# Seven tile products for eight in the second product of two chunks of a sequence transform

## The chip, the cores and the metric

One core of one Trainium2 chip. The metric is the device time of one execution, in microseconds; before the change it is 792.81 us (median of three runs, 792.65 to 792.82). Names of engines: PE is TensorE (matmuls), DVE VectorE, ACT ScalarE, POOL GpSimd, SP SyncE, which only issues DMAs here.

## The reference

```python
def reference(A_x, A_dft_seq_re, A_dft_seq_im, A_dft_hid_re, A_dft_hid_im, B_x, B_w_gate, B_w_up, B_w_down):
    xn = _layernorm(x, axis=-1)                              # x = A_x, 2048 x 512
    a = einsum("bsd,ed->bse", xn, dft_hid_re);  b = einsum("bsd,ed->bse", xn, dft_hid_im)
    s = einsum("ts,bse->bte", dft_seq_re, a) - einsum("ts,bse->bte", dft_seq_im, b)
    h = sigmoid(xn @ w_gate) * (xn @ w_up)                   # 512 -> 1792
    g = silu(h @ w_down)                                     # 1792 -> 512
    return x + s * g
```

The sequence transforms are 2048x2048, the hidden ones 512x512, all in float32.

## The kernel before

**Arithmetic.** Each operand is split into a high part (a copy on ACT in a reduced float32 form, line 119) and a low part (the difference, on DVE, line 124). A tile product takes three matmuls, high by high, high by low and low by high, in `mm3` (lines 67 to 71); line 68 sets their order, and `late` puts the one with the low part of the moving operand third. Matrix products are made by a scheme of seven products for eight: products 1 and 2 take raw blocks, products 5, 6, 7 and 4 sums of blocks, product 3 a raw block against a sum. `combine` (line 127) makes the sums on DVE.

**Stages.** First the sequence transform of the normalised x, in four chunks of 512 output positions (class `Chunk`, made in `begin_seq`), which writes the blocks `f_raw[t][0..3]` in DRAM; then the GLU in fourteen blocks (`block`, `Down`), whose partial results add up in DRAM (`g_part`); last the hidden transform (`hidden_units`), which reads `f_raw` and sums of it (`f_sum`, made by `f_sums`), multiplies by the gate and writes the output.

**Units.** Work is a list of units, most of them 12 matmuls of 128x512. Ahead of unit n the loop at the end of the kernel asks for the loads of the units up to n + 5 (`LOAD_AHEAD`), and makes the splits of those up to n + 2 (`SPLIT_AHEAD`). What else is to happen stands in tables by unit number: `sooner` (ahead of the unit's loads), `amid` (behind its splits), `after` (behind its matmuls). Each engine runs its own instructions in the order in which this loop writes them. SBUF is 54 pages of 4 KB a partition, taken in turn: a load on SP's queue waits until the page it gets has been read for the last time.

**PSUM.** Banks go by tags: ga, ua, gb, ub, gc, uc, and two called pd.

**The transform.** The units of product 1 for pp 0 to 3 take the four chunks in turn, then those of product 2 (16 units each). Then each chunk does its products 5, 6, 7, 3 and 4, four units each (`add_product`). Product 1 is copied out by `snap` and stands in a bank again for the chain of 6, 7 and 4 (`again`, line 285); product 2 is copied out and added by a sum of the two blocks in PSUM, and `put` writes it. Products 5 and 3, and 6 and 7, meet in `join` (line 320): DVE subtracts one from a copy of the other and the result is written once. The sums of blocks of the transform matrix (t1 to t4) are made by DVE; in chunk 0 t1 and t3 are a `Sum`: a load, and a DMA on POOL's queue that adds the second block to it in SBUF (line 232). The second half of x (rows j = 1) is fetched (line 155), measured (`stats`, whose scale is made by POOL in lines 167 to 169) and normalised (line 186) while product 2 runs, and `a_sums` makes its sums.

**The GLU.** `w_operands` makes the seven operands from the gate and up weights, each 128x512, and splits each by itself; `Down` keeps four sums of blocks in one page.

## Time and profile before

| | before |
|---|---|
| time, median of three runs | 792.81 us (792.65 to 792.82) |
| span of the profiled execution | 790.8 us |
| busy PE, DVE, ACT, POOL | 786.3, 670.1, 520.9, 148.6 us |
| matmuls | 3466 |
| bytes moved over the span | 190.46 MB, mean 241 GB/s |
| DMA packets under 512 B | 6208 of 56306 |

The span goes from the first to the last instruction of the profiled execution. A row of a grouped view reads: line, engine, operation, written tile <- read tile, partitions x elements and type, count, then busy time and the mean of one, then the idle time of that engine just ahead, and what ended it. A row of a timeline: start, duration, the same names, and in brackets the idle time ahead of it with its releaser. A row of the chain: start, length, engine, tile and line. A row of the waits: who waits <- for whom, then total us, how often, and the longest. A row of the windows: the window, then for PE, its weight loads, DVE, ACT and POOL the busy time, the granted clock, the mean busy share of the DMA engines and GB/s. A row of the DMAs: line, tiles and count, bytes, and the issue times.

### The profile page before, as it was taken

The numbers are of one execution on the slowest core, as the hardware profiler recorded it, in microseconds if no ns is written. First come the engines' busy times: TensorE is split into PE (matmuls) and PEld (weight loads), VectorE is DVE, ScalarE is ACT, GpSimd is POOL, SyncE is SP. The second block draws the span as 40 slices with busy tenths as digits, with TensorE's granted clock in tenths as the row PEclk, the third lists the DMA queues.
The fourth block names the chain that finished last, engine by engine and source line by source line (L and its number), as shares of the span: only waits on it lengthen the run. The fifth ranks groups of instructions, "written<-read, shape, count | busy, mean of one in ns | idle before, by whom it ended". The sixth has DMA issues, their size and how long they took to land.

```text
span 790.8 us, 9957 instructions
## 1 busy us (share of the span) xinstructions
PE 786.3 (99%) x3466; PEld 650.8 (82%) x3466; DVE 670.1 (85%) x881; ACT 520.9 (66%) x795; POOL 148.6 (19%) x199
## 2 busy tenths in 40 slices
PE   9999999999999999999999999999999999999998
PEld 7888888888888888888888888888888888888886
DVE  6877799978899989899999888668869898896967
ACT  6787575552543555677887767576577787887571
POOL 3525300000021002022111131122222111111301
PEclk9999999999999999999999999999999999999999
DMA  9994988357699446859976996799999898999996
GB/s 345 409 380 124 312 241 278 120 197 279 256 274 361 160 163 224 227 165 229 201 128 96 228 228 186 220 207 294 286 299 265 186 226 219 237 285 316 268 348 169
DMA packets 56306, 190.46 MB, mean 241 GB/s; under 512 B 6208, under 2 KB 6720, under 8 KB 56256
## 3 DMA queue, kind: packets, MB, share of 16 engines
q0 software_dynamic: 23360, 77.62, 45.5%
q1 hardware_dynamic: 32896, 112.21, 38.9%
q8 instruction: 27, 0.44, 0.2%
q14 instruction: 23, 0.19, 0.1%
HBM read 122.68 MB, written 70.27 MB: 244 GB/s over the span
## 4 chain that ended last, share of the span: by engine, by line
PE 99%; DVE 0%; issue 0%
PE pd L71 30%; PE ga L71 15%; PE ua L71 15%; PE uc L71 10%; PE gc L71 10%; PE gb L71 9%; PE ub L71 9%; PE pd L417 0%; PE gb L417 0%; PE ub L417 0%; DVE page L883 0%; DVE page L884 0%
## 5 line engine op out<-in xcount | busy, mean ns | idle before, releaser
L124 DVE TENSOR_TENSOR page<-page 128x512 fp32r<-128x512 f32 (+1 forms) x378 | 343.1, 938 | 69.8 <-ACT page L119 68.5
L119 ACT ACTIVATE page<-page 128x512 fp32r<-128x512 f32 (+1 forms) x378 | 297.2, 829 | 108.0 <-DVE page L128 95.5
L71 PE MATMUL pd<-page 128*128 128x512 f32 x1068 | 259.5, 388 | 0.0
L71 PEld LDWEIGHTS pd<-page 128*128 128x128 f32 x1068 | 199.8, 188 | 41.2
L128 DVE TENSOR_TENSOR page<-page 128x1024 f32<-128x1024 f32 (+2 forms) x244 | 195.4, 820 | 1.2 <-DMA page<-in_w_gu_dram 0.3
L71 PE MATMUL ga<-page 128*128 128x512 f32 x528 | 139.1, 390 | 0.0
L71 PE MATMUL ua<-page 128*128 128x512 f32 x528 | 138.8, 389 | 0.0
L71 PEld LDWEIGHTS ga<-page 128*128 128x128 f32 x528 | 99.3, 188 | 21.4 <-ACT page L363 0.7
L71 PEld LDWEIGHTS ua<-page 128*128 128x128 f32 x528 | 99.4, 188 | 20.6
L559 POOL DMA_DIRECT2D g_part<-page x76 | 66.2, 871 | 265.4 <-ACT page L568 159.9
L568 ACT ACTIVATE page<-pd 128x512 f32<-128x512 f32 x140 | 82.4, 598 | 24.7 <-PE pd L71 17.4
L71 PE MATMUL gc<-page 128*128 128x512 f32 x336 | 88.3, 389 | 0.0
L71 PE MATMUL uc<-page 128*128 128x512 f32 x336 | 88.3, 389 | 0.0
L71 PE MATMUL gb<-page 128*128 128x512 f32 (+1 forms) x336 | 86.8, 385 | 0.0
L71 PE MATMUL ub<-page 128*128 128x512 f32 x324 | 85.3, 389 | 0.0
L71 PEld LDWEIGHTS uc<-page 128*128 128x128 f32 x336 | 63.1, 188 | 13.1
L71 PEld LDWEIGHTS gc<-page 128*128 128x128 f32 x336 | 63.1, 188 | 13.1
L71 PEld LDWEIGHTS gb<-page 128*128 128x128 f32 x336 | 62.2, 188 | 12.6
L71 PEld LDWEIGHTS ub<-page 128*128 128x128 f32 x324 | 60.8, 188 | 12.6
L308 POOL DMA_DIRECT2D f_raw<-page x16 | 9.0, 564 | 190.2 <-DVE page L320 137.5
L676 ACT ACTIVATE page<-ga 128x512 f32<-128x512 f32 x28 | 16.6, 593 | 17.4 <-PE ga L71 13.3
L694 DVE TENSOR_TENSOR page<-page 128x512 f32<-128x512 f32 x28 | 19.3, 689 | 10.0 <-ACT page L691 9.3
(105 smaller groups left out, 392.5 us busy)
## 6 DMA issues: line engine op xcount, KB each, us to landing
g_part<-page POOLq DMA_DIRECT2D x84, 512.0 KB, 7.4
page<-in_c_re_dram SPq DMA_DIRECT2D x60, 512.0 KB, 7.5
page<-in_c_im_dram SPq DMA_DIRECT2D x32, 512.0 KB, 6.2
page<-f_raw SPq DMA_DIRECT2D x28, 512.0 KB, 7.4
page<-in_w_gu_dram SPq DMA_DIRECT2D x22, 512.0 KB, 6.5
f_raw<-page POOLq DMA_DIRECT2D x16, 512.0 KB, 5.8
f_sum<-page POOLq DMA_DIRECT2D x16, 512.0 KB, 7.3
page<-f_sum SPq DMA_DIRECT2D x16, 512.0 KB, 9.9
```

The source lines that it names most:

```text
L71: nc.tensor.matmul(ps, ws[w], ms[m], start=first and i == 0, stop=last and i == 2, skip_group_check=go_on)
L119: nc.scalar.activation(self.parts[0], self.raw, AF.Copy)
L124: nc.vector.tensor_tensor(lo, self.raw, hi.bitcast(F32), op=SUB)
L128: (engine or nc.vector).tensor_tensor(dst, a, b, op=op)
L308: nc.gpsimd.dma_start(f_raw[self.t][block], v)
L559: nc.gpsimd.dma_start(g_part[i], pg, accum_op=ADD)
L568: nc.scalar.activation(pg[:, o, :], po, AF.Copy, scale=float(sign))
L676: nc.scalar.activation(s[k][:, m, :], ps[c + "a"], AF.Copy)
L694: nc.vector.tensor_mul(s[k][:, 0, :], s[k][:, 0, :], ps["u" + tag] if tag else s[k][:, 1, :])
```

## The change

In the transform, product 2 of chunks 2 and 3 (`PAIR`) leaves the units of `Chunk`. Two groups `Inner` do it for both chunks together: one group for pp 0 and 1, one for pp 2 and 3, each with seven products of 2 x 3 matmuls. The products stand as units of six matmuls, two by two behind every second unit of products 6, 7, 3 and 4: the first group between the units of chunk 1, the second between those of chunk 2, in banks that the chunk doesn't use. Each group loads x and its four blocks of the matrix again, normalises and sums x, and makes the sums of its blocks. Chunks 2 and 3 write product 1 as block 0, and the groups add to it in DRAM by accumulating DMAs. Of all chunks products 5, 6, 7, 3 and 4 are now each copied out by ACT; 5 and 6 write blocks 3 and 2, products 7 and 3 are added to these by accumulating DMAs, and `join` is gone. t3 is a `Sum` in every chunk. With eight units fewer at the start, fetch, statistics, normalisation and sums of the second half of x stand closer together. In the GLU six of seven weight operands are split two at a time, as 1024, through `Piece`; `Down` keeps three sums in a page and one in place; and the first `f_sums`, in steps of two units ahead of the GLU, go to its later part, in steps of one.

```diff
+    class Piece(Value):
+
+
+        def __init__(self, whole, of):
+            super().__init__([whole], None)
+            self.whole, self.of, self.begin, self.high = whole, of, whole.begin, whole.high
+
+        def get(self):
+            return [self.of(v) for v in self.whole.get()]
...
+    PAIR = 2, 3
...
-                t3 = Value([b22], onto(b12.load, b22.load)) if t else Sum(b12, b22)
+                t3 = Sum(b12, b22)
...
-        def put(self, block, v):
-            nc.gpsimd.dma_start(f_raw[self.t][block], v)
-
...
-        def join(self, block, name, ch, swap=False):
-            v = self.s[name]
-            for d in range(2):
-                a, b = v[:, d, :], self.ps[ch, d]
-                nc.vector.tensor_tensor(v[:, d, :], *((b, a) if swap else (a, b)), op=SUB)
-            self.put(block, v)
+                nc.scalar.activation(v[:, d, :], self.ps[ch, d], AF.Copy, scale=float(sign))
+            return v
 
         def done(self, k):
             if k < 3:
-                v = self.snap(f"p{k}", "p")
-                if k == 2:
+                v = self.s[f"p{k}"] = self.snap("p")
+                if k == (1 if self.t in PAIR else 2):
                     self.put(0, v)
...
             else:
-                self.put(1, self.snap("u4", "a"))
-
-        def add_product(self, k):
-            total = (9, 3) if self.t == 0 and k in (5, 7) else (6, 3)
+                block, ch, sign, onto = {5: (3, "c", -1, False), 6: (2, "a", 1, False), 7: (3, "a", 1, True), 3: (2, "c", -1, True), 4: (1, "a", 1, False)}[k]
+                self.put(block, self.snap(ch, sign), onto)
+
+        def add_product(self, k, between=()):
+            between = list(between)
+            total = (9, 3) if isinstance(self.total.get((k, 0)), Sum) else (6, 3)
...
+                if pp % 2 and between:
+                    between.pop(0)()
+
+    class Inner:
+
+
+        ORDER = 1, 5, 6, 3, 2, 7, 4
+
+        def __init__(self, pps, tags):
+            self.pps, self.tags, self.ps, self.a = pps, tags, {}, None
+            self.x = Load(None, None)
+            self.x.load = self.x.get = self.load_x
+            self.b = {(i, e): Load(None, None) for i in range(2) for e in range(2)}
+            for (i, e), v in self.b.items():
+                v.load = v.get = lambda i=i, e=e: self.load_b(i, e)
+            b11, b21, b12, b22 = (self.b[v].load for v in ((0, 0), (0, 1), (1, 0), (1, 1)))
+            self.raw = Parts([], self.x.load, [2, 2, D // 2])
+            self.sum = Parts([], lambda: self.s, [2, 4, P])
+            t1 = Value([], lambda: combine(b11(), b12(), b11(), SUB))
+            t3 = Value([], lambda: combine(b12(), b22(), b12(), SUB))
+            t2 = Value([], lambda: combine(t1.get(), b22(), t1.get(), SUB))
+            t4 = Value([], lambda: combine(t2.get(), b21(), t2.get(), SUB))
+            self.total = {5: t1, 6: t2, 7: t3, 4: t4}
+            src = {1: b11, 2: b21, 3: b22, 5: t1.get, 6: t2.get, 7: t3.get, 4: t4.get}
+            self.op = {k: Parts([], v, [2, SB]) for k, v in src.items()}
+
...
+        def load_b(self, i, e):
+            v = self.b[i, e]
+            if v.at is None:
+                v.at = page([2, SB], F32)
+                for q, pp in enumerate(self.pps):
+                    nc.sync.dma_start(v.at[:, q, :], c_re[1, pp, PAIR[i]][:, e, :])
+            return v.at
+
...
+        def sums(self, n):
+            v = self.x.load()
+            a11, a12, a21, a22 = (v[:, :, e, d * P : (d + 1) * P] for d in range(2) for e in range(2))
+            if n == 0:
+                self.s = page([2, 4, P], F32)
+                combine(self.s[:, :, 0, :], a21, a22, ADD)
+                combine(self.s[:, :, 1, :], self.s[:, :, 0, :], a11, SUB)
+            else:
+                combine(self.s[:, :, 2, :], a11, a21, SUB)
+                combine(self.s[:, :, 3, :], a12, self.s[:, :, 1, :], SUB)
+
...
+        def run(self, k):
+            at, first = {1: (21, True), 5: (12, True), 6: (21, False), 3: (12, False), 2: (11, False), 7: (21, False), 4: (21, False)}[k]
+            if first:
+                self.ps[at] = bank(self.tags[at])
+            if k == 1:
+                self.ps[11] = bank(self.tags[11])
+            ps, m = self.ps[at], self.op[k].get()
+            for q in range(2):
+                mm3(ps, self.weights(k, q), [v[:, q, :] for v in m], first and q == 0, q == 1, not first, True)
+            if k == 1:
+                nc.scalar.activation(self.ps[11], ps, AF.Copy)
+            elif k == 5:
+                self.out = page([2, SB], F32)
+                nc.scalar.activation(self.out[:, 1, :], ps, AF.Copy)
+            elif k == 6:
+                nc.scalar.activation(self.out[:, 0, :], ps, AF.Copy)
+            elif k == 3:
+                nc.vector.tensor_tensor(self.out[:, 0, :], self.out[:, 0, :], ps, op=ADD)
+            elif k == 7:
+                nc.vector.tensor_tensor(self.out[:, 1, :], self.out[:, 1, :], ps, op=ADD)
+                nc.gpsimd.dma_start(f_raw[PAIR[1]][0], self.out, accum_op=ADD)
+            elif k == 4:
+                v = page([2, SB], F32)
+                for d, at in enumerate((11, 21)):
+                    nc.scalar.activation(v[:, d, :], self.ps[at], AF.Copy)
+                nc.gpsimd.dma_start(f_raw[PAIR[0]][0], v, accum_op=ADD)
+
+        def add(self, k):
+            m = len(units)
+            if k == self.ORDER[0]:
+                sooner(m - 9, self.x.load)
+                for v in self.b.values():
+                    sooner(m - 7, v.load)
+                sooner(m - 5, self.normed)
+                sooner(m - 4, lambda: self.sums(0))
+                sooner(m - 3, lambda: self.sums(1))
+            if k in self.total:
+                sooner(m - 2, self.total[k].get)
+            add(self.needs(k), lambda: self.run(k))
...
-                m = NT * (4 * i + pp)
-                for c in chunks:
+                m = len(units)
+                for c in chunks[: 2 if i else NT]:
...
-                    sooner(m - 11, lambda pp=pp: fetch(1, pp))
-                    after((9, 12, 16, 20)[pp], lambda pp=pp: stats(1, pp))
-                    after((11, 14, 18, 22)[pp], lambda pp=pp: normalise(1, pp))
+                    sooner((5, 7, 9, 11)[pp], lambda pp=pp: fetch(1, pp))
+                    after((9, 11, 13, 15)[pp], lambda pp=pp: stats(1, pp))
+                    after((11, 13, 15, 17)[pp], lambda pp=pp: normalise(1, pp))
...
-            after((13, 17, 21, 24)[pp], lambda pp=pp: a_sums(pp, (1,)))
-            after((15, 19, 23, 26)[pp], aop[5, pp].get)
-            for s, at in {3: 28, 2: 30, 4: 36}.items():
+            after((13, 15, 17, 19)[pp], lambda pp=pp: a_sums(pp, (1,)))
+            after((15, 17, 19, 21)[pp], aop[5, pp].get)
+            for s, at in {3: 20, 2: 22, 4: 28}.items():
                 after(at + pp, lambda pp=pp, s=s: a_sums(pp, (s,)))
+        inner = Inner((0, 1), {21: "ga", 11: "ua", 12: "gb"}), Inner((2, 3), {21: "gc", 11: "uc", 12: "pd"})
         for c in chunks:
-            for k in (5, 6, 7, 3, 4):
-                c.add_product(k)
+            steps = [lambda v=v, k=k: v.add(k) for v in inner[c.t - 1 : c.t] for k in v.ORDER] if c.t in (1, 2) else []
+            c.add_product(5)
+            for k in (6, 7, 3, 4):
+                c.add_product(k, steps[:2])
+                del steps[:2]
...
-        two = [Value([], lambda: page([2, 4 * P], F32)) for _ in range(2)]
-
...
+        two = Value([], lambda: page([2, 4 * P], F32))
+
+        def made(to, a, b, op):
+            return Value(loads, lambda: combine(to(), a(), b(), op))
+
+        s1 = made(lambda: two.get()[:, 0, :], raw(1, 0), raw(1, 1), ADD)
+        s2 = made(lambda: two.get()[:, 1, :], s1.get, raw(0, 0), SUB)
+        s3 = made(raw(1, 0), raw(0, 0), raw(1, 0), SUB)
+        s4 = made(raw(0, 1), raw(0, 1), s2.get, SUB)
+        w = {3: Parts(loads, s4.get, [4 * P], joint=True)}
+        for ks, v in ((1, 2), loads[0].load), ((5, 6), two.get), ((4, 7), loads[1].load):
+            whole = Parts(loads, v, [2, 4 * P])
+            for i, k in enumerate(ks):
+                w[k] = Piece(whole, lambda v, i=i: v[:, i, :])
...
-                    t.append(page([4, D // 2], F32))
+                    t.append(page([3, D // 2], F32))
                     combine(t[0][:, 0, :], quarter(0, 1), quarter(1, 1), SUB)
                     combine(t[0][:, 1, :], t[0][:, 0, :], quarter(0, 0), SUB)
                 else:
-                    combine(t[0][:, 2, :], quarter(0, 0), quarter(0, 1), SUB)
-                    combine(t[0][:, 3, :], quarter(1, 0), t[0][:, 1, :], ADD)
+                    combine(quarter(0, 1), quarter(0, 0), quarter(0, 1), SUB)
+                    combine(t[0][:, 2, :], quarter(1, 0), t[0][:, 1, :], ADD)
...
-            return [self.h[k], self.dif if k in (5, 6, 7, 3) else self.raw]
+            return [self.h[k], self.dif if k in (5, 6, 3) else self.raw]
...
-            for i, v in zip((-3, 0, 1, 3), w["s"]):
+            for i, v in zip((-3, -2, 1, 3), w["s"]):
...
-        f_sums(0, 0, n - 38, 2)
         f_sums(0, 1, n + 38, 1)
         f_sums(1, 0, n + 54, 1)
         f_sums(1, 1, n + 70, 1)
+        f_sums(0, 0, n + 78, 1)
```

On TensorE, at the start of the second product, before (ga and ua are chunk 0, gb and ub chunk 1, gc and uc chunk 2, pd chunk 3; the fourth row begins chunk 1):

```order
L71 MATMUL ua<-page 128x512 x2
L71 MATMUL ga<-page 128x512 x2
L71 MATMUL ua<-page 128x512 x2
L71 MATMUL gb<-page 128x512 x2
L71 MATMUL ub<-page 128x512 x2
L71 MATMUL gb<-page 128x512 x2
L71 MATMUL ub<-page 128x512 x2
L71 MATMUL gb<-page 128x512 x2
L71 MATMUL ub<-page 128x512 x2
L71 MATMUL gc<-page 128x512 x2
L71 MATMUL uc<-page 128x512 x2
```

And now:

```order
L71 MATMUL ua<-page 128x512 x2
L71 MATMUL ga<-page 128x512 x2
L71 MATMUL ua<-page 128x512 x2
L71 MATMUL gb<-page 128x512 x2
L71 MATMUL ub<-page 128x512 x2
L71 MATMUL gb<-page 128x512 x2
L71 MATMUL ub<-page 128x512 x2
L71 MATMUL gb<-page 128x512 x2
L71 MATMUL ub<-page 128x512 x2
L71 MATMUL ga<-page 128x512 x2
L71 MATMUL ua<-page 128x512 x2
```

Behind chunk 1's unit stands the next unit of chunk 0, no longer chunks 2 and 3.

On ScalarE, at the end of product 1 in chunk 3 (whose banks are pd), before: the copies out of the bank, one split of x (512), one of the matrix (1024), a normalisation of the first half of x.

```order
L119 ACTIVATE page<-page 128x1024
L313 ACTIVATE page<-pd 128x512 x2
L119 ACTIVATE page<-page 128x512
L119 ACTIVATE page<-page 128x1024
L186 ACTIVATE page<-page,moments 128x256 x2
```

And now:

```order
L119 ACTIVATE page<-page 128x1024
L324 ACTIVATE page<-pd 128x512 x2
L196 ACTIVATE page<-page,moments 128x512 x2
L119 ACTIVATE page<-page 128x512 x2
L119 ACTIVATE page<-page 128x1024
L196 ACTIVATE page<-page,moments 128x256 x2
```

A normalisation of the second half of x and another split of x stand ahead of the same split of the matrix.

On VectorE, at the end of chunk 2, before (ga and ua are the banks of its product 3, line 320 its join, line 128 the sums for the next units, line 124 the low parts, line 517 the step of the x normalisation for the GLU):

```order
L320 TENSOR_TENSOR page<-page,ga 128x512
L320 TENSOR_TENSOR page<-page,ua 128x512
L128 TENSOR_TENSOR page<-page 128x1024
L124 TENSOR_TENSOR page<-page 128x1024
L517 TENSOR_TENSOR page<-page 128x1024
L128 TENSOR_TENSOR page<-page 128x1024
L124 TENSOR_TENSOR page<-page 128x1024
```

And now (gc is the bank of the second group's product 7, line 433 its add, line 138 the sums, line 625 the step of the x normalisation):

```order
L433 TENSOR_TENSOR page<-page,gc 128x512
L138 TENSOR_TENSOR page<-page 128x1024 x2
L124 TENSOR_TENSOR page<-page 128x1024
L138 TENSOR_TENSOR page<-page 128x1024
L124 TENSOR_TENSOR page<-page 128x1024
L625 TENSOR_TENSOR page<-page 128x1024
L138 TENSOR_TENSOR page<-page 128x1024
L124 TENSOR_TENSOR page<-page 128x1024
```

The join is gone. Where two operations of 512 and five of 1024 stood up to the last split shown, there are now one of 512 and eight of 1024.

50 lines of the change are left out of this document (26 added, 24 removed).

## The prediction

> **What bounds the kernel now.** I read the page first: its head and its clock line, then the chain that ended last and the waits of PE.
>
> ```profile
> span 790.8 us, 9957 instructions
> PE 786.3 (99%) x3466; PEld 650.8 (82%) x3466; DVE 670.1 (85%) x881; ACT 520.9 (66%) x795; POOL 148.6 (19%) x199
> ...
> PEclk9999999999999999999999999999999999999999
> ...
> PE 99%; DVE 0%; issue 0%
> ```
> ```profile
> PE gb L417 <- PEq L1007: 0.8, 1, 0.8
> ```
> ```profile
> 47.15 2.72 PE pd L71 x12
> ...
> 267.47 21.76 PE pd L71 x96
> ```
>
> TensorE is the chain, at full clock. The waits view knows one wait of PE in the whole run, 0.8 us before its first instruction. The last fence is from the chain: 96 matmuls in 21.76 us, so one each 226.7 ns, and a unit of the transform (12 matmuls) each 2.72 us. There is no hole to fill: time falls only with the count of matmuls, and rises with every operand that comes late. So the question is what the change takes off that count, and whether VectorE, ScalarE and the DMAs still deliver.
>
> The profiled span is 790.8 us, the median of the runs 792.81 us: 2.0 us lie outside the span, and I carry them over unchanged.
>
> **What is removed on TensorE.** For chunks 2 and 3 the second product took 4 units each, 8 x 12 = 96 matmuls. In its place come two groups of seven products with 2 x 3 matmuls each, 2 x 7 x 6 = 84. All else on PE is the same: 3466 records before, 12 fewer after. The new matmuls have the same 128x512 form, and six in a row into one bank is what the row of 96 above does, so the same price holds: 12 x 0.2267 = 2.72 us. A matmul that started a new bank at a worse price would have to show in these chain rows, and none does; so I give this term no spread. **The sum: 790.8 - 2.72 = 788.1 us of span, 790.1 us of time.** That is also the floor; all other edits can only leave it or add.
>
> **What is added and taken away beside PE.** The rows that price it (grouped by form; the second last number is busy time, the last the mean):
>
> ```profile
> L124 DVE TENSOR_TENSOR page<-page 128x1024 fp32r<-128x1024 f32 x179 | 216.2, 1219 | 43.1 <-ACT page L119 42.9
> L119 ACT ACTIVATE page<-page 128x1024 fp32r<-128x1024 f32 x179 | 184.1, 1054 | 77.9 <-DVE page L128 76.4 <-DMA page<-in_c_re_dram 0.6 <-DMA page<-f_raw 0.4
> L124 DVE TENSOR_TENSOR page<-page 128x512 fp32r<-128x512 f32 x199 | 131.7, 685 | 26.7 <-ACT page L119 25.5
> L128 DVE TENSOR_TENSOR page<-page 128x1024 f32<-128x1024 f32 x84 | 101.9, 1217 | 0.0
> L128 DVE TENSOR_TENSOR page<-page 128x256 f32<-128x256 f32 x44 | 17.5, 419 | 0.4
> L320 DVE TENSOR_TENSOR page<-pd,page 128x512 f32<-128x512 f32 x4 | 2.8, 690 | 4.6 <-PE pd L71 4.6
> ```
>
> VectorE in the transform loses 16 joins (16 x 0.69 = 11.0 us), 8 splits of the removed units (8 x 1.219 = 9.8) and 12 sums that become accumulating DMAs (12 x 1.217 = 14.6). It gains 18 splits (18 x 1.219 = 21.9), 8 sums of c blocks (9.7), 8 sums of x, for which no row has the form 2x128 and which I take at the 128x256 row (3.4; between 3.4 and 5.5 if they cost as 512), and 4 adds from PSUM (2.8): 35.4 us go, 37.8 come. Behind the transform 66 splits of 512 become 33 of 1024 (45.2 to 40.2 us), and 11 of 1024 become 768 (between 0.685 and 1.219 us; about 0.95, so 3 us less). None of this is on PE's chain. ScalarE gets 7 instructions more; at 66% I cost it at nothing, with the queue check below. The move of the first f_raw sums to a later stage takes four sums (4.9 us) and eight transfers out of the transform and sets them among weight blocks, where DVE loses 8 us.
>
> All this is free only as long as each unit's split is ready. So the budget is checked at the two densest places.
>
> **First place: the eight units taken out of the start.** The second product now runs two chunks instead of four, so statistics and normalisation of the second half of x come each 5.4 us, not each 11 us.
>
> In ScalarE's rows shown with the change, a normalisation and one split of x moved ahead of the last 1024 split, the one for the third unit of the second product. Its time, from ScalarE's timeline of before, whose order up to the first of these rows gives the same end:
>
> ```profile
> 47.80 1.55 ACT L186 ACTIVATE page<-page,moments 128x512 f32<-128x512 f32 x2
> 49.22 1.08 ACT L119 ACTIVATE page<-page 128x1024 fp32r<-128x1024 f32 x1
> 50.17 1.10 ACT L313 ACTIVATE page<-pd 128x512 f32<-128x512 f32 x2
> 51.12 1.62 ACT L119 ACTIVATE page<-page 128x512 fp32r<-128x512 f32 x2
> ```
>
> By the starts: two copies 0.95 us, normalisation 1.42, a 512 split 0.52, a 1024 split 0.95. From 50.17: 0.95 + 1.42 + 2 x 0.52 + 0.95 = 4.36, so the split is done at 54.5 us. The unit before the second product ends at 47.15 + 2.72 = 49.87 (chain row above), the third unit starts 5.44 later, at 55.3. Spare: 0.8 us. Two units later the last normalisation waits for POOL:
>
> ```profile
> 44.34 0.70 POOL L167 TENSOR_TENSOR moments<-rs,mhalf 128x2 f32<-128x2 f32 x1 [5.73 <-DVE rs L166]
> ...
> 45.92 0.52 POOL L169 TENSOR_TENSOR moments<-moments 128x2 f32<-128x2 f32 x1
> ...
> 55.97 1.60 POOL L167 TENSOR_TENSOR moments<-rs,mhalf 128x2 f32<-128x2 f32 x1 [9.52 <-DVE rs L166]
> ...
> 58.36 1.06 POOL L169 TENSOR_TENSOR moments<-moments 128x2 f32<-128x2 f32 x1
> ```
>
> ```profile
> 42.28 0.69 DVE L173 BATCH_NORM_STATS2 st<-page 128x6 f32<-128x512 f32 x1
> ...
> 44.09 0.17 DVE L166 TENSOR_SCALAR rs<-mv 128x2 f32<-128x2 f32 x1
> ...
> 50.33 1.23 DVE L124 TENSOR_TENSOR page<-page 128x1024 fp32r<-128x1024 f32 x1 [2.10 <-ACT page L119]
> 51.82 0.69 DVE L124 TENSOR_TENSOR page<-page 128x512 fp32r<-128x512 f32 x1 [0.27 <-ACT page L119]
> ```
>
> That chain takes 2.1 us (44.34 to 46.44) to 3.45 us (55.97 to 59.42). The statistics ahead of it now stand right behind the split that began at 50.33: 1.14 for the split and 1.98 for two blocks (42.28 to 44.26) put their end at an estimated 53.45. So POOL ends between 55.55 and 56.9; with 1.42 + 2 x 0.52 + 0.95 the split comes between 58.95 and 60.3, against a unit start at 49.87 + 4 x 2.72 = 60.75. Spare 0.45 to 1.8 us. I take both as held, stall 0; the other end is about 1 us if the chain takes a microsecond more than its longest.
>
> The Trainium skill, "SBUF — State Buffer", section "Who interferes with whom", says that a VectorE instruction with two inputs in SBUF contends with a GpSimd instruction that reads SBUF, which speaks against packing both closer. By it the longer chain is the one to expect; the two lengths above agree with such a thing without showing it, and the sum stays, as 60.3 is before 60.75.
>
> **Second place: the end of chunk 2, where the second group of seven, the x normalisation and chunk 3's first sums meet.** In VectorE's rows shown with the change, one add and eight operations of 1024 stand from product 7's end to the last split shown. That split belongs to chunk 2's last unit. Between the end of product 7 and that unit PE now runs 12 + 12 + 6 + 12 = 42 matmuls, 9.52 us. VectorE's pace, from its timeline:
>
> ```profile
> 245.75 0.69 DVE L320 TENSOR_TENSOR page<-page,ua 128x512 f32<-128x512 f32 x1 [0.51 <-PE ua L71]
> 246.35 1.22 DVE L128 TENSOR_TENSOR page<-page 128x1024 f32<-128x1024 f32 x1
> ...
> 249.76 1.22 DVE L128 TENSOR_TENSOR page<-page 128x1024 f32<-128x1024 f32 x1
> 250.90 1.22 DVE L124 TENSOR_TENSOR page<-page 128x1024 fp32r<-128x1024 f32 x1
> ```
>
> By the starts a 512 takes 0.60 us and a 1024 takes 1.14. One add and eight of 1024: 0.60 + 8 x 1.14 = 9.7 us. That is 0.2 late against the unit's first matmul, and the low part is first read by its third matmul (line 68), 0.45 later: spare 0.2 us, less about 0.1 to 0.3 that VectorE sees product 7's end late. I take **0.1 us** of stall. The units behind need 2.27 us of each 2.72, so it does not pile up. Bounds: 0 and, if VectorE comes to the add a full unit late, 2.7 us.
>
> **Sum:** 790.1 + 0.1 = 790.2 us.
>
> **Rivals.** *Queues just too slow (0.27).* Both places have under 1 us to spare, and the group in chunk 1 has its own. If VectorE or ScalarE is late by 0.5 to 1 us at three of them, 1.5 to 3 us come back: 792.3 us. For it: these spares. Against: windows of 20 us in which VectorE was busy 97% and PE still did not wait:
>
> ```profile
> 100.00:120.00 20.00, 20.00 (x90) 16.54 (x89) 19.44 (x23) 14.27 (x21) 0.88 (x1) 1.00 0.83 229
> ...
> 240.00:260.00 20.00, 20.00 (x90) 16.57 (x89) 19.07 (x19) 8.40 (x9) 2.38 (x3) 1.00 1.05 352
> ```
>
> *Chunk 3's blocks land late (0.15): slower.* SP's loads wait for free pages (54), and a group of seven holds about ten (x, four blocks, sums, two pairs of splits, an output) through most of a chunk.
>
> ```profile
> SPq L80 <- DVE page L124: 175.7, 39, 21.1
> ```
> ```profile
> L80 SPq DMA_DIRECT2D page<-in_c_im_dram x8: 328/328/443, 236.7 to 248.5; - x8
> ...
> DMA to landing us min/median/max: 6.4/11.2/17.0
> ```
>
> The second fence is line 80 from 228 to 250 us, at a DMA share of 1.05 (window row above). The first of these blocks was issued at 236.7 and read at 249.76: 13.1 us ahead, with a median landing of 11.2, 1.9 spare. A unit uses up about three pages; ten fewer put the issue up to three units, 8 us, later. If half of that holds at the start of chunks 2 and 3, each loses 4 - 1.9 = 2.1 us or, at the full 8, 6.1: 4 to 12 us, and nearest to the low end, as the group's blocks come free before its end, about 5: 795 us. It decides from the point where issue to use falls under the landing plus 3 us for sum and split. Chunk 2's start has the lighter traffic, so both are needed for slower than 0.2%.
>
> The Trainium skill, "DMA: Bandwidth & Descriptors", section "Issuing engines are not separate DMA queues", says that transfers from all issuers share the same 16 DMA engines. It speaks for this rival: 24 more accumulating transfers on POOL's queue do not run beside SP's loads but among them. The DMA share of 1.05 agrees. By the fit of the same page (section "Anatomy of one DMA") an accumulate of 512 KB would be an estimated 3.2 us; the row of before says
>
> ```profile
> DMA to landing us min/median/max: 8.5/11.6/20.3
> ```
>
> (line 232), and the sum goes by the row: they are asked for nine units, 24.5 us, ahead, which covers 20.3 barely.
>
> *The change doesn't do what it says:* the count of matmuls rules it out.
>
> **How the numbers follow.** The forecast, all 12 matmuls and stalls under 1 us, gets 0.58; the queues 0.27; the late loads 0.15. A difference of 0.2%, 1.6 us, is about what a measurement of this kernel can tell from none: faster is under 791.2, slower over 794.4, so the three cases are the three chances. The range runs from the floor, 789.9 with 0.2 for the runs' spread, to 793.7, which leaves out the late loads and the worst of the queues.
>
> **What would show it.** Right: 3454 matmuls, PE with no wait past its start, a span near 788.1. First place wrong: PE waiting for ACT L119 between 55 and 65 us. Second place wrong: PE waiting for DVE L124 some 2 to 3 units ahead of chunk 3. Late loads: ACT L119 or DVE L138 idle for DMA page<-in_c_im_dram at 180 to 195 or 245 to 262 us. A hole anywhere behind 310 us would make the prediction wrong for a reason not seen here.

## The result and the profile after

The changed kernel takes **814.92 us** (median of 4 runs, 812.79 to 816.71), the kernel before 792.82 beside it: a ratio of 1.0277, 95% interval 1.0255 to 1.0299. It is 22 us slower. The forecast was 790.2 us. The profiled execution is the fastest of the four, at 812.79 us.

The head of the page after, its queues and its chain:

```profile
span 810.9 us, 10003 instructions
PE 790.9 (98%) x3454; PEld 649.4 (80%) x3454; DVE 667.4 (82%) x850; ACT 539.4 (67%) x802; POOL 167.2 (21%) x223
PE   9999999999899699999999999999999999999998
PEclk9999999999999899999999999999999999999999
q0 software_dynamic: 26816, 90.21, 52.8%
q1 hardware_dynamic: 35136, 113.26, 37.8%
PE 89%; DMA 5%; DVE 3%; issue 1%; ACT 1%; SPq 0%; DVEq 0%; ACTq 0%
```

The 12 matmuls are gone (3466 to 3454), as the change says. But TensorE is no longer the whole chain: a transfer stands in it with 5%, where before there was none. Two of the 40 slices have a large hole, at about 205 and 265 us, and the second has a lower clock (the row PEclk, the granted clock of TensorE in tenths). The rows of the waits view that matter, of TensorE and of VectorE:

```profile
PE gc L71 <- DVE page L124: 10.6, 5, 3.3
PE pd L71 <- DVE page L124: 2.6, 4, 0.8
PE gb L71 <- DVE page L124: 1.0, 2, 0.6
DVE page L138 <- DMA page<-in_c_im_dram: 20.9, 8, 6.5
```

TensorE waits for low parts (line 124), and these wait behind sums (line 138) for blocks of the transform matrix on their way from DRAM. VectorE's timeline at the two holes:

```profile
201.16 1.22 DVE L124 TENSOR_TENSOR page<-page 128x1024 fp32r<-128x1024 f32 x1
208.91 1.23 DVE L138 TENSOR_TENSOR page<-page 128x1024 f32<-128x1024 f32 x1 [6.54 <-DMA page<-in_c_im_dram]
210.05 2.35 DVE L124 TENSOR_TENSOR page<-page 128x1024 fp32r<-128x1024 f32 x2
...
262.98 1.23 DVE L138 TENSOR_TENSOR page<-page 128x1024 f32<-128x1024 f32 x1 [2.46 <-DMA page<-in_c_im_dram]
...
269.17 1.23 DVE L138 TENSOR_TENSOR page<-page 128x1024 f32<-128x1024 f32 x1 [3.82 <-DMA page<-in_c_im_dram]
...
276.35 1.22 DVE L138 TENSOR_TENSOR page<-page 128x1024 f32<-128x1024 f32 x1 [4.82 <-DMA page<-in_c_im_dram]
```

At chunk 2's first units one block is 6.5 us late. At chunk 3's, block after block is late. To compare kernels I add up the holes: for each two matmuls in a row, the distance of their starts over 0.227 us, where it is over 0.235 us. The sums so hold the matmuls that run at a lower clock behind a wait, too.

| holes of PE, us | start, to 20 us | 20 to 200 | 200 to 235 (chunk 2) | 235 to 300 (chunk 3) | behind 300 |
|---|---|---|---|---|---|
| before | 3.1 | 0 | 0 | 0 | 0 |
| after | 3.3 | 1.4 | 6.1 | 14.5 | 0.2 |

The start is the same. So the profiled execution has 22 us of new holes on top of the forecast span: 788.1 + 22.2 = 810.3, against a span of 810.9. All but 0.2 us of them lie in the transform.

The loads that are late are the eight blocks `in_c_im` among the issues of line 80 around chunk 3's start. After (the second row is over all 14 loads of the line in this window, as in the prediction):

```profile
L80 SPq DMA_DIRECT2D page<-in_c_im_dram x8: 328/328/383, 243.5 to 263.0; - x8
DMA to landing us min/median/max: 8.5/19.6/27.2
```

Two things differ from before. The eight blocks are issued over 19.5 us, not 11.8. And the median landing is 19.6 us, not 11.2. The second comes first in time: the first two blocks were issued 14.7 us ahead of the time when VectorE was ready for them, no later than before (13.1 and 14.2 us), but took 13.7 and 17.0 us to land, against 6.4 and 10.1. The next two took 20.7 and 24.7 us, against 11.6 and 14.9.

The DMA engines are full from 240 to 280 us (the columns behind the window are PE, its weight loads, DVE, ACT, POOL, clock, DMA share, GB/s):

```profile
240.00:260.00 20.00, 19.38 (x85) 15.45 (x84) 19.73 (x19) 9.01 (x11) 3.26 (x5) 1.00 1.06 281
260.00:280.00 20.00, 12.94 (x42) 9.20 (x42) 8.63 (x8) 4.63 (x6) 4.58 (x6) 0.83 1.06 309
```

Before, they were as full from 220 to 260 us (1.02 and 1.05), but moved more, 352 GB/s from 240 to 260, and from 260 us on the share fell to 0.42:

```profile
260.00:280.00 20.00, 20.00 (x89) 16.54 (x89) 17.72 (x17) 10.56 (x14) 0.00 (x0) 1.00 0.42 148
```

What fills them differs. Of the 16 engines' time from 240 to 265 us, POOL's queue (q0, with the accumulating transfers) takes this much, before and after (packets, MB, share):

```profile
q0 software_dynamic: 865, 2.20, 34.9%
q0 software_dynamic: 1018, 2.79, 59.8%
```

### The profile page after: what moved, and what is told of

It reads as the page before. It is cut to its first block, busy times and chain, and to the rows that moved or that the text cites. A ratio compares the mean times of both kernels' runs of the same rounds, so it can differ in the third digit from the quotient of the medians.

```text
span 810.9 us, 10003 instructions
## 1 busy us (share of the span) xinstructions
PE 790.9 (98%) x3454; PEld 649.4 (80%) x3454; DVE 667.4 (82%) x850; ACT 539.4 (67%) x802; POOL 167.2 (21%) x223
## 3 DMA queue, kind: packets, MB, share of 16 engines
q0 software_dynamic: 26816, 90.21, 52.8%
## 4 chain that ended last, share of the span: by engine, by line
PE 89%; DMA 5%; DVE 3%; issue 1%; ACT 1%; SPq 0%; DVEq 0%; ACTq 0%
PE pd L71 27%; PE ga L71 14%; PE ua L71 14%; PE gb L71 9%; PE gc L71 8%; PE uc L71 8%; PE ub L71 8%; DMA page<-in_c_im_dram 5%; DVE page L124 2%; DVE page L138 1%; DMA page<-in_c_re_dram 0%; ACT page L119 0%; DVE page L433 0%; ACT page L438 0%; SPq L533 0%
## 5 line engine op out<-in xcount | busy, mean ns | idle before, releaser
L124 DVE TENSOR_TENSOR page<-page 128x1024 fp32r<-128x1024 f32 (+1 forms) x355 | 348.4, 1011 | 88.0 <-ACT page L119 83.5
L119 ACT ACTIVATE page<-page 128x1024 fp32r<-128x1024 f32 (+1 forms) x355 | 299.9, 887 | 113.2 <-DVE page L138 93.1
L71 PE MATMUL pd<-page 128*128 128x512 f32 (+1 forms) x1032 | 253.0, 388 | 2.6 <-DVE page L124 2.6
L71 PEld LDWEIGHTS pd<-page 128*128 128x128 f32 x1032 | 192.8, 188 | 44.1 <-DVE page L124 4.3
L138 DVE TENSOR_TENSOR page<-page 128x1024 f32<-128x1024 f32 (+2 forms) x248 | 194.1, 801 | 22.0 <-DMA page<-in_c_im_dram 20.9
L71 PE MATMUL ga<-page 128*128 128x512 f32 x552 | 144.9, 389 | 1.0 <-ACT page L467 1.0
L71 PEld LDWEIGHTS ga<-page 128*128 128x128 f32 x552 | 103.5, 188 | 23.4 <-ACT page L467 1.4
L71 PEld LDWEIGHTS ua<-page 128*128 128x128 f32 x534 | 100.2, 188 | 20.7
L71 PE MATMUL gb<-page 128*128 128x512 f32 (+1 forms) x348 | 91.7, 389 | 1.0 <-DVE page L124 1.0
L71 PE MATMUL uc<-page 128*128 128x512 f32 x318 | 83.7, 394 | 0.0
L319 POOL DMA_DIRECT2D f_raw<-page x24 | 16.9, 702 | 200.7 <-ACT page L324 181.1
L787 ACT ACTIVATE page<-ua 128x512 f32<-128x512 f32 x28 | 16.8, 598 | 15.6 <-PE ua L71 15.6
L787 ACT ACTIVATE page<-ga 128x512 f32<-128x512 f32 x28 | 16.6, 595 | 14.9 <-PE ga L71 14.5
```

The costliest lines, as they stand in the source:

```text
L71: nc.tensor.matmul(ps, ws[w], ms[m], start=first and i == 0, stop=last and i == 2, skip_group_check=go_on)
L119: nc.scalar.activation(self.parts[0], self.raw, AF.Copy)
L124: nc.vector.tensor_tensor(lo, self.raw, hi.bitcast(F32), op=SUB)
L138: (engine or nc.vector).tensor_tensor(dst, a, b, op=op)
L319: nc.gpsimd.dma_start(f_raw[self.t][block], v, **({"accum_op": ADD} if onto else {}))
L787: nc.scalar.activation(s[k][:, m, :], ps[c + "a"], AF.Copy)
```

## The experiments

The question was what makes these loads late. Four things are new at that place: accumulating transfers for t3, accumulating transfers in place of the joins, the groups' bytes, and the groups' pages of SBUF. Each run is timed beside the kernel before (792.1 to 792.6 us). The holes are those of its profiled execution.

### One part at a time

**t3 back on VectorE.**

```diff
-                t3 = Sum(b12, b22)
+                t3 = Value([b22], onto(b12.load, b22.load)) if t else Sum(b12, b22)
```

> The changed kernel with one edit undone: the sums t3 of chunks 1 to 3 are made by VectorE again, not by accumulating DMAs (12 of the 24 new accumulating transfers go, 12 VectorE sums of 1.14 us come). Theory 'traffic': the new accumulating transfers fill the DMA engines (share 1.05 at 185 to 212 and 240 to 292 us), and SP's loads of the transform matrix land late behind them; half of them and all that run beside chunk 3's loads are gone, so the time falls from 815 to 790 to 798 us and the holes behind 256 us go. Theory 'pages': the two groups of seven use up pages, so loads are issued later; the DMA engines are not what is short; the time stays at 808 us or above. Theory 'VectorE': with 13.7 us more on VectorE, PE waits for DVE at the ends of chunks without a load being late: 795 to 805.

Measured: 805.22 us (801.99 to 808.29). 9.7 us come back in the median. The profiled execution, the slowest of the four, still has holes of 1.9 us at chunk 2 (6.1 in the changed kernel) and 11.0 at chunk 3 (14.5). So t3's transfers are a part, and not the cause alone.

**t3 by DMA in the kernel before**, and nothing else.

> The kernel before with one edit of the change alone: t3 of chunks 1 to 3 by accumulating DMAs, asked for nine units ahead as in the change. No group of seven, same matmuls. Traffic: four more accumulating transfers stand beside chunk 3's loads, which in the kernel before land only 1.2 to 1.6 us ahead of their use (255 to 262 us); at 2.85 us of all 16 DMA engines for each (428.2 less 359.8 us of the software queue's share over 24 more transfers) that is 11 us of DMA work, and the time rises to 796 to 803 us with the holes at 255 to 285 us. Pages: 792.5 to 794 us, no hole over 0.5 us.

Measured: 792.75 us, ratio 1.0014 (0.9999 to 1.0028), no hole behind the start. The forecast of "traffic" is wrong: twelve more accumulating transfers alone cost nothing that is clear of the noise, which is wide here (the ten runs go from 792.27 to 797.13, the kernel before beside them from 792.08 to 794.68). Its page prices them: the software queue takes 49.3% of 790.6 us, 389.8 us, where it took 45.5% of 790.8, 359.8. That is 30 us, 2.5 us of all 16 engines for each 512 KB.

**The joins back on VectorE**, with the groups and t3 as in the change (the core; `join` itself as before).

```diff
-                block, ch, sign, onto = {5: (3, "c", -1, False), 6: (2, "a", 1, False), 7: (3, "a", 1, True), 3: (2, "c", -1, True), 4: (1, "a", 1, False)}[k]
-                self.put(block, self.snap(ch, sign), onto)
+            elif k == 3:
+                self.join(2, "u2", "c")
+            elif k == 7:
+                self.join(3, "u5", "a", swap=True)
```

> The changed kernel with another edit undone: products 5 and 3, and 6 and 7 meet on VectorE again and each result is written once, so eight of the 24 accumulating transfers and none of the plain ones go; VectorE gets 16 operations of 0.60 us. t3 and the groups stay. Traffic: a third of the added work goes, of which about three transfers stand in the two saturated stretches: 803 to 811 us. Pages: no load is issued earlier, 812 to 817 us.

Measured: 808.59 us (807.20 to 810.94), holes 7.9 us at chunk 2 and 8.7 at chunk 3. 6.3 us come back, at chunk 3: the hole at chunk 2 has not become smaller.

**Both back on VectorE.**

> The changed kernel with t3 of chunks 1 to 3 and the joins both back on VectorE: 20 of the 24 accumulating transfers gone, the groups stay. By the two single undoings (805.2 and 808.6 against 814.9 us) the sum of the gains would be 16.0 us: 798.9 us. If the accumulating transfers are what makes loads late: 793 to 800. If the groups' pages alone suffice: 800 to 806, holes still ahead of and in chunk 3, now partly as a wait for VectorE, which has 25 us more work.

Measured: 798.42 us (794.95 to 798.98). The gains add up nearly as the sum said (798.9). Holes in the profiled execution, which was the fastest: 0.8 at chunk 2, 2.9 at chunk 3. 8 us over the floor of 790.1 remain in the median, with the groups.

**The groups left out.**

```diff
-            steps = [lambda v=v, k=k: v.add(k) for v in inner[c.t - 1 : c.t] for k in v.ORDER] if c.t in (1, 2) else []
+            steps = []
```

> The changed kernel with both groups of seven left out: the second product of chunks 2 and 3 is not computed at all, nor are its loads and its four accumulating transfers; t3 and the joins stay as DMAs. 84 matmuls fewer take 19.0 us from the floor: 790.1 becomes 771.1 us. Pages: without the groups the loads are issued as early as before, and the time is 771 to 774 us. Traffic: of the 24 accumulating transfers 20 stay, and PE's time beside them gets shorter, so most of the holes stay: 777 to 790 us.

This kernel leaves out the second product of chunks 2 and 3. Measured: 771.06 us (770.61 to 772.88), the floor without the groups, 771.1, and no hole over 0.4 us behind the start. Twenty accumulating transfers, the tighter start, the moved f_raw sums and the GLU's wider splits cost nothing there. Without groups no load makes TensorE wait. The page of this kernel on the same loads, issued for chunk 3:

```profile
L80 SPq DMA_DIRECT2D page<-in_c_im_dram x8: 328/328/782, 207.2 to 226.2; - x8
DMA to landing us min/median/max: 4.2/11.4/18.2
```

Here the issues lie as far apart as in the changed kernel (19 us), but the first stands 22 us ahead of VectorE's use of it (229.4), where the changed kernel has 15 (243.5 to 258.2). The median landing is 11.4 us, as before.

### Bytes or pages

Both kernels leave the groups out, so part of the result is not computed, and put back one of their two burdens, beside the twenty accumulating transfers that stay. In both the stand-ins are issued on SP's queue several in a row, so each also has some of what the order in that queue costs; and the stand-ins for the bytes go from DRAM to DRAM, where the groups' loads go to SBUF. Bytes (the core; the blocks, x alike):

```diff
+                            for e in range(2):
+                                nc.sync.dma_start(spare[g][4 * i + 2 * q + e][:, 0, :], c_re[1, 2 * g + q, PAIR[i]][:, e, :])
...
+                for i, at in enumerate((10, 14)):
+                    after(m + at, lambda i=i, g=g: nc.gpsimd.dma_start(spare[g][10 + i], c_re[1, i, g]))
```

> The changed kernel without the groups (their part of the second product is not computed) but with their transfers: at the same places SP copies the same pieces of x and of the matrix from DRAM to DRAM, and POOL's queue two blocks of 512 KB, so the DMA engines have the groups' bytes and no page of SBUF is taken. Without these copies the same kernel took 771.1 us with no hole. Theory 'traffic': the groups' bytes on top of the accumulating transfers are what is too much, and holes come back: 776 to 790 us. Theory 'pages': bytes alone do nothing: 771 to 773 us.

Pages:

```diff
+                    for _ in range(9):
+                        kept.append(page([2, SB], F32))
+                        nc.sync.dma_start(kept[-1][:, 0, :2], x[0, 1][:, 0, :2])
...
+                    for v in kept:
+                        nc.gpsimd.tensor_tensor(held, v[:, 0, :2], minus, op=ALU.mult)
```

> The changed kernel without the groups (their part of the second product is not computed) but with their pages: in chunks 1 and 2 nine pages, about what a group holds at once (x sums, four blocks, two pairs of splits, an output), are taken five units ahead of product 6 by a transfer of 1 KB each and given back behind product 4's third unit. No other bytes, no sums, no splits. Pages: loads wait longer for a page and land late at the starts of chunks 2 and 3: 775 to 788 us. Traffic: 771 to 773 us.

Measured: bytes alone 781.16 us (779.37 to 784.24), pages alone 780.70 (779.69 to 781.96). Each costs about 10 us over 771.06, so neither theory was right to give the other nothing. The holes differ in place. With bytes they stand in all three chunks (2.4 us in chunk 1, 4.0 in chunk 2, 2.3 in chunk 3). With pages 9.2 us stand at chunk 3. The loads of that kernel there (its line numbers are one higher):

```profile
L81 SPq DMA_DIRECT2D page<-in_c_im_dram x8: 327/328/526, 217.1 to 233.1; - x8
DMA to landing us min/median/max: 6.1/13.4/24.8
```

VectorE wants the first block at 229.3 us, as in the kernel without groups (229.4), but it is issued 12 us ahead, not 22. So held pages take away the lead. In the changed kernel the last five of the eight blocks are issued over 11.8 us, where the kernel before, first row, takes 8.7:

```profile
240.08 8.71 SPq L80 DMA_DIRECT2D page<-in_c_im_dram  x5
251.51 11.77 SPq L80 DMA_DIRECT2D page<-in_c_im_dram  x5
```

SP's waits in the changed kernel from 240 to 264 us say for what:

```profile
SPq L80 <- DMA f_raw<-page: 9.2, 2, 6.2
```

The two transfers that it waited for add chunk 2's product 3 and the second group's product 7 in DRAM; they were done with their pages at 258.1 and 261.9 us, and the next blocks left within 0.5 us of that. Before, there is no such wait at this place, but 7.5 us for two transfers of f_sum. So accumulating transfers that take long hold pages too, and bytes and pages are not two separate burdens.

**Four pages fewer in the kernel before.**

```diff
-PAGES = 54
+PAGES = 50
```

> The kernel before with 50 pages, not 54; nothing else. Pages: a load is issued when a page comes free, and chunk 3's blocks landed 1.2 to 1.6 us ahead of their use; a unit takes 3 to 4 pages, so four fewer put issues about one unit, 2.7 us, later: holes of 1 to 5 us in all at 250 to 265 us, 794 to 798 us. If pages are not short at that place: 792.1 to 793 us, and no hole there.

Measured: 813.81 us (813.47 to 814.09). The size is four times what was expected, and the place is another: no hole at 250 us, 20.9 us of holes behind 400 us, nearly all in the GLU. The kernel before has no page to spare, but at chunk 3's start four fewer do not show.

### When and where the groups ask

**Products closer together.** One behind each unit of products 7 and 3.

```diff
-                if pp % 2 and between:
+                if between:
...
-                c.add_product(k, steps[:2])
-                del steps[:2]
+                n = 4 if k in (7, 3) else 0
+                c.add_product(k, steps[:n])
+                del steps[:n]
```

> The changed kernel with the groups' products one behind each unit of products 7 and 3, not one behind every second unit of 6, 7, 3 and 4. Same work and bytes; a group holds its pages for some eight units fewer and has given them back when the next chunk's first loads want theirs. Pages: 794 to 804 us, with the holes at the chunks' starts smaller. Traffic: the same transfers in less time, 812 to 820 us. VectorE has 2.9 us of work in each 4.1 us there, so no wait for it alone.

Measured: 811.61 us (810.20 to 812.50): 3 us less, in neither forecast range, with holes of 16.0 us between 235 and 300 us. Shorter holding, with the same transfers in less time, is not enough.

**The second group in chunk 3.**

```diff
-        inner = Inner((0, 1), {21: "ga", 11: "ua", 12: "gb"}), Inner((2, 3), {21: "gc", 11: "uc", 12: "pd"})
+        inner = Inner((0, 1), {21: "ga", 11: "ua", 12: "gb"}), Inner((2, 3), {21: "ga", 11: "ua", 12: "gb"})
...
-            steps = [lambda v=v, k=k: v.add(k) for v in inner[c.t - 1 : c.t] for k in v.ORDER] if c.t in (1, 2) else []
+            steps = [lambda v=v, k=k: v.add(k) for v in inner[c.t // 2 : c.t // 2 + 1] for k in v.ORDER] if c.t in (1, 3) else []
```

> The changed kernel with the second group between chunk 3's units (banks ga, ua, gb), not chunk 2's. Same matmuls, same transfers, 0 accumulating transfers fewer. Chunk 2 now has neither a group's pages nor its loads, and the loads for chunk 3 meet only the accumulating transfers, which alone cost nothing (no groups: 771.1 us without a hole). Theory 'pages and bytes together': the holes at 250 to 292 us (about 17 us) go, and that at 207 us (about 4 us), where the second group's own loads stood, gets smaller: 791 to 798 us. Theory 'VectorE': the group's 18.9 us of VectorE work on top of 42.5 in chunk 3's 63.9 us is too dense beside the first operands of the GLU: 796 to 804 us with PE waiting for DVE at 265 to 320 us and no load late.

Measured: 813.26 us (811.09 to 814.41). Both theories miss the size. The hole at chunk 2 is gone, as expected, but chunk 3 has 14.9 us again, and VectorE adds 5.6 behind 300 us. With the joins of two chunks (as above, for chunks 1 and 2) and t3 of one on VectorE:

```diff
-                t3 = Sum(b12, b22)
+                t3 = Value([b22], onto(b12.load, b22.load)) if t == 2 else Sum(b12, b22)
```

> The kernel with the second group in chunk 3, and besides the joins of chunks 1 and 2 and t3 of chunk 2 back on VectorE (8 accumulating transfers fewer, 7.7 us more for VectorE, all of it ahead of chunk 3). If what is left at the starts of chunks 2 and 3 are late loads, they get earlier: 790.2 to 793 us, and 1 to 4 us under the kernel with the group in chunk 3 alone. If what is left is VectorE in chunk 3, no change against that kernel.

Measured: 808.80 us (807.37 to 809.66), 4.5 us less, but far from 790.2 to 793, with one hole of 9 us at 261 us (9.4 us from one matmul's start to the next). Looking at what was issued ahead of the late block showed something that I had not thought of. SP issues a group's four blocks in one go, and three of them are read much later. In the changed kernel, SP's timeline at the first hole:

```profile
187.42 7.66 SPq L385 DMA_DIRECT2D page<-in_c_re_dram  x8
196.09 0.99 SPq L80 DMA_DIRECT2D page<-in_c_im_dram  x2
```

Line 385 loads the second group's blocks, eight pieces; three of the four blocks are needed by TensorE at 220, 227 and 241 us. Of the two blocks of the chunk behind them, VectorE was ready to add the first at 202.4 us; it landed at 208.9. The low parts for the group's first product stand behind that sum in VectorE's order, and TensorE stood still for them from 208.0 us.

**Blocks asked for when due.**

```diff
-                for v in self.b.values():
-                    sooner(m - 7, v.load)
+                sooner(m - 7, self.b[0, 0].load)
...
+            if k in (5, 6, 2):
+                sooner(m - 7, self.b[{5: (1, 0), 6: (1, 1), 2: (0, 1)}[k]].load)
```

> The changed kernel with one edit: a group's four blocks of the matrix are asked for seven units ahead of the product whose operand first needs each, not all four seven units ahead of the group's first product. Same transfers, same work. In the changed kernel three of the second group's blocks, needed 31 to 52 us later, stand in SP's queue ahead of two blocks of the chunk, needed 15 to 18 us later. Theory 'order and holding': the hole at 207 us (about 6 us with the slow clock behind it) goes, and since a block is held for up to 13 units less, loads for chunk 3 are issued earlier: 798 to 808 us. Theory 'bytes': the same transfers must pass, 812 to 817 us.

Measured: 807.27 us (806.38 to 808.51). The same transfers, and 7.7 us less. The hole at chunk 2 is gone to the last tenth (6.1 to 0), with the DMA share at 1.01 there:

```profile
200.00:220.00 20.00, 20.00 (x90) 16.57 (x89) 16.56 (x17) 12.62 (x16) 4.06 (x5) 1.00 1.01 290
```

So the first hole was the order in SP's queue, which decides what gets the next free page, and not how full the engines are. But chunk 3 keeps its 14.4 us: there asking later for the groups' blocks changes nothing.

The same edit on the kernel with t3 and the joins on VectorE:

> The kernel with t3 and the joins on VectorE (798.4 us), and the blocks asked for when due. If the holes left there are late loads: 790.5 to 794 us; if they are VectorE, which has 25 us more than in the changed kernel: 796 to 799 us.

Measured: 798.45 us (795.45 to 800.04): no change, and inside the range for VectorE. But its trace, of the slowest run, has 5.8 us of holes from 235 to 300 us. The largest hole at chunk 3, 2.4 us, still stands behind a late block, and the 1.5 us at the end of chunk 2 are VectorE's. So it is some of both.

And on the kernel with the second group in chunk 3:

> The kernel with the second group in chunk 3 and part of the sums on VectorE (808.8 us), and the blocks asked for when due. There one hole of 9.4 us at 261 us stands where two blocks of chunk 3 landed behind eight pieces for the group that were needed 10 to 45 us later. Order: that hole goes, 796 to 801 us, the holes of 5 us at 310 to 320 us (VectorE) stay. Bytes: 806 to 810 us.

Measured: 799.14 us (798.59 to 801.63), as expected: the 9.4 us hole is gone. 4.2 us of small holes at 235 to 300 us are left, and 4.9 from 300 to 400 us are VectorE, which runs there without a gap:

```profile
302.08 1.22 DVE L124 TENSOR_TENSOR page<-page 128x1024 fp32r<-128x1024 f32 x1
303.21 0.68 DVE L449 TENSOR_TENSOR page<-page,ga 128x512 f32<-128x512 f32 x1
303.81 2.36 DVE L138 TENSOR_TENSOR page<-page 128x1024 f32<-128x1024 f32 x2
306.16 1.23 DVE L124 TENSOR_TENSOR page<-page 128x1024 fp32r<-128x1024 f32 x1
```

**Other bytes moved:** the broadcast transfers for the GLU's x, six units later.

```diff
-        x_norm(0, 0, (n - 30, n - 27))
-        x_norm(0, 1, (n - 24, n - 18))
+        x_norm(0, 0, (n - 24, n - 21))
+        x_norm(0, 1, (n - 18, n - 13))
```

The first of the two has this on the kernel with t3 on VectorE, the joins of chunks 0 to 2 too, and the blocks when due; the second on the changed kernel with the blocks when due.

> The kernel with t3 and the joins on VectorE and the blocks asked for when due (798.5 us), with two edits: the broadcast accumulating transfers and multiplications that make the GLU's x in chunk 3 stand six units later (the last five), and chunk 3's joins are left to the DMAs. If bytes beside chunk 3's first loads are what is left of the late loads (issued at 234 to 257 us, 13 to 19 us to landing), the holes of 4 to 5 us at 252 to 268 us go: 791 to 795 us. If pages alone set it, no change: 797 to 799 us; if VectorE gets too dense in chunk 3: 798 to 803 us with waits for it at 280 to 310 us.

> The changed kernel with the blocks asked for when due (807.3 us) and those broadcast transfers six units later; t3 and the joins stay accumulating transfers. Bytes: four transfers of 512 KB with their loads leave the place where chunk 3's loads queue, some 10 us of DMA work; the holes of 13 us at 250 to 275 us shrink to about half: 799 to 803 us. Pages alone: 805 to 809 us.

Measured: 799.73 us (799.03 to 801.10), against 798.45 without the two edits, and 805.47 us (805.18 to 805.89) against 807.27. So the move brought 2 us in the changed kernel and none in the other. It doesn't settle what these bytes cost, since it did not take them away from the late loads. In the changed kernel with the blocks when due, the eight blocks of chunk 3 are issued from 237 to 257 us; one of the four broadcast transfers is issued in that stretch without the edit (the others at 216, 230 and 230 us), and two with it (246 and 253; the others at 230 and 273). The DMA share from 260 to 280 us is 1.06 in both. None of the kernels with the whole second product beats the kernel before.

## Why the prediction was wrong

**The step that failed** is the sum's stall: it holds 0.1 us for VectorE and nothing for blocks of the matrix that land late. The budget was made for what VectorE and ScalarE have to do, at two places; for the loads, the time from issue to landing was held at 11.2 us, and a delay was left to a rival. In the profiled execution late blocks cost about 19 of the 22.2 us of new holes (6.1 at chunk 2, some 13 at chunk 3, slow matmuls behind them included), and waits for VectorE at the ends of chunks the other 3.

**TensorE's count was right.** 12 x 0.2267 us is in the sum as it was forecast; the kernel without groups, at 771.06, shows the price of 84 more and that no other edit outside the groups costs anything by itself.

**The first dense place was right.** ScalarE's rows after:

```profile
51.23 1.55 ACT L196 ACTIVATE page<-page,moments 128x512 f32<-128x512 f32 x2
52.64 2.12 ACT L119 ACTIVATE page<-page 128x512 fp32r<-128x512 f32 x3
...
56.57 1.53 ACT L196 ACTIVATE page<-page,moments 128x512 f32<-128x512 f32 x2
58.00 3.56 ACT L119 ACTIVATE page<-page 128x512 fp32r<-128x512 f32 x5
```

The second row is two splits of 512 and the one of 1024 that was put at 54.5 us; it ends at 54.8. The last normalisation starts at 56.57, inside the 55.55 to 56.9 for POOL's end. TensorE does not wait there: 20 to 75 us has no hole.

**The second dense place was right in kind and too small.** I took 0.1 us; the holes at the last two units of chunk 2 are 0.8 and 0.6 us, and the end of chunk 1 has 0.8 (0.9 with the matmul behind it). What was too small is that VectorE would see product 7's end 0.1 to 0.3 us late:

```profile
247.76 1.52 PE L71 MATMUL gc<-page 128*128 128x512 f32 x6
...
249.54 1.23 DVE L124 TENSOR_TENSOR page<-page 128x1024 fp32r<-128x1024 f32 x1 [0.22 <-ACT page L119]
250.68 0.68 DVE L433 TENSOR_TENSOR page<-page,gc 128x512 f32<-128x512 f32 x1
```

The product ends at 249.28, the add starts at 250.68: 1.4 us late, behind a split that waited for ScalarE.

**The rival "chunk 3's blocks land late" is what happened**, at 0.15 and priced at 5 us where about 19 came. It had the places right, both chunk starts, and the accumulating transfers on POOL's queue among SP's loads. Its mechanism was half right: it let issues come later, and at chunk 3 the first blocks were not issued later but took longer to land. Its size failed in four steps.

1. The landing was held at its median of 11.2 us, with only the issue moving. It went to 19.6, and to 27.2 for the last. Nor was the first block the one with the least to spare: in the kernel before it landed 6.7 us ahead of its use (243.0 and 249.8 us), the fifth 1.3 us (258.1 and 259.4). I priced the accumulating transfers as VectorE's gain and never added them to the DMA engines. The queue rows give it: the software queue took 359.8 us of 16 engines before, and takes 52.8% of 810.9, 428.2, after; 68.4 us for 24 transfers. The kernel without groups shows that twenty of them are free by themselves, and the one with t3 and the joins on VectorE that, with groups, 16.5 us hang on these twenty.
2. The delay was taken once for each chunk. In chunk 3 the waits come again at each unit, since each next block lands as far behind.
3. I thought of the groups' pages, but not of the order of SP's queue: 6.1 us at chunk 2 are blocks asked for 31 to 52 us ahead of need in front of a block that VectorE was ready for 6 us after its issue.
4. TensorE runs at half speed behind some holes, below: 16 matmuls at 0.427 us behind the two longest, 3.2 us more than at full clock.

The Trainium skill, "DMA: Bandwidth & Descriptors", section "Issuing engines are not separate DMA queues", says, as the prediction has it, that all issuers share 16 engines. The runs agree, and show when this costs: twelve more transfers alone cost nothing (792.75 us), twenty without the groups nothing either (771.06), and the groups' bytes on top of these, with no page held, 10 us (781.16).

**The other edits** (wider splits, `Down`, `f_sums` later) cost nothing: 0.2 us of holes behind 300 us. The rival of queues that are just too slow, at 0.27 and 1.5 to 3 us, is about 3 us of the 22, so it came true as well.

**What stays open** is how chunk 3's 14.5 us divide between pages and bytes. Beside the twenty accumulating transfers, the groups' bytes give 2.3 there and their pages 9.2; the transfers alone give 0; and with the groups but without these twenty, 2.9 are left in the fastest execution and 5.8 in another (there with the blocks asked for when due). They do not add up, so they condition each other. No kernel with more than 54 pages was run; one would tell.

## What to carry to other kernels

A change that takes a few matmuls off a full TensorE must be charged for its transfers and its buffers as carefully as for its instructions: add up the DMA engines' time by queue, stage by stage, and look at issue to landing and at landing to use for the loads with the least to spare. Where loads wait for free buffers, transfers that cost nothing by themselves can cost much beside something that holds buffers and adds bytes: here 0 and 16.5 us for the same twenty, where the change could gain 2.7. And ask for a block when it is due: a load that is asked for early takes its place in the queue from one that is urgent.

## What the hardware showed

**The clock falls behind a hole.** TensorE's rows at chunk 3's start:

```profile
265.40 1.20 PE L71 MATMUL gc<-page 128*128 128x512 f32 x4 [1.81 <-DVE page L124]
266.43 1.53 PE L71 MATMUL uc<-page 128*128 128x512 f32 x6
...
271.58 2.08 PE L71 MATMUL gc<-page 128*128 128x512 f32 x4 [3.17 <-DVE page L124]
273.45 2.76 PE L71 MATMUL uc<-page 128*128 128x512 f32 x6
```

After a wait of 1.81 us the next six take their old time; after one of 3.17 us they take 2.76 us instead of 1.53, 0.427 us each by their starts. The granted clock of the window from 271.58 to 276 us is 0.50. The Trainium skill, "TensorE: Matmul & The Clock Gate", section "Part 1: The HAM clock gate", puts the change to the slow state at an idle window of about 3.4 us, and the way back at as much sustained work. The trace agrees on the length: the clock is at half for 3.41 us from 212.5 and for 6.83, twice that, from 270.5. It does not agree that the whole 3.4 us must be idle. Here the clock fell about 2 us into the wait, and in the kernel with pages alone a wait of 1.80 us was enough:

```profile
247.55 1.78 PE L72 MATMUL gc<-page 128*128 128x512 f32 x4 [1.80 <-DVE page L125]
249.13 2.56 PE L72 MATMUL uc<-page 128*128 128x512 f32 x6
```

Waits of 2.66 us (the kernel before with 50 pages, at 466 us) and 2.29 us (the first kernel with the transfers moved, at 270 us) had no slow matmul behind them. Every hole over 3 us behind the start, in any of these traces, had some. Ten slow matmuls, as behind the wait of 3.17 us, cost 2 us more than at full clock.

**An accumulating transfer of 512 KB takes 2.5 to 2.85 us of all 16 DMA engines** (30.0 us for 12, 68.4 for 24), a plain load on SP's queue 1.4 (38.9% of 790.8 us for 112.21 MB), all counted by the time of their packets in the queue rows.

**Four pages of 54 are worth 21 us** to the kernel before, in the GLU, and none at the place where I looked for it.
